# Attention and two gated projections on one core: padding that moves where the SBUF buffers begin

## Chip, cores and metric

The kernel runs on one core of a Trainium2 chip. The metric is the device time of one launch in microseconds (us), the median of the runs shown.

## What is computed

Attention over 2 batches and 8 heads of 768 positions, each position seeing the 31 positions around it and a summary of every block of 32 (the maximum of the block's keys, the mean of its values); then two dense stages, all of it in float32:

```
scores = concat(where(|i-j| < 16, q k^T / 8, -1e9), q max_blocks(k)^T / 8 + log 32)
x  = softmax(scores) @ concat(v, mean_blocks(v))      # 1536 x 512
y  = ((x @ w_a) * (x @ w_b)) @ w_out                  # 512 -> 1536 -> 512
h  = y @ w_in                                         # 512 -> 2048
out = (h - tanh(h)) @ w_out2                          # 2048 -> 512
```

## The kernel before

**Tiles and stages.** The 1536 tokens are three blocks (`NBLK`) of `TB` = 512. Batch 0's attention is written out operation by operation in the list `SEQ` (a head of some 40 us, run by `op`); batch 1's attention is spread by a plan (`plan`, `run_plan`) between the matmuls of the first dense stage. The program is then a list of positions, `pos`: for each block and each of the 12 slices of the first hidden layer, `pos_a` (x @ w_a), `pos_b` (x @ w_b) and `pos_o` (the product @ w_out), and for each block and each of the 16 slices of the second hidden layer `pos_h` (y @ w_in and the function h - tanh h) and, two positions later, `pos_o2` (its product with w_out2). Every position is one unit of 12 matmuls: 4 pieces of 128 by 3 products, since each float32 number is held as a high and a low part (`hi_lo`, `split_w`) and high*high, high*low and low*high are added up. So there are 36 units each of `pos_a`, `pos_b` and `pos_o`, and 48 each of `pos_h` and `pos_o2`.

**What a matmul reads.** Both operands lie in SBUF; one is loaded as weights (stationary, 128 columns, 512 bytes in a partition), the other streams through (moving, 512 columns, 2048 bytes).

- `proj` (L370; called by `pos_a`, `pos_b`, `pos_h`): stationary from `wsp`, moving from `XA` or `XB`.
- `pos_o` (L398): stationary from `wsp`, moving from `gh` or `gl`.
- `pos_o2` (L459): stationary from `gh` and `gl` in two units of three and from `vw` in the third (`G % 3`), moving from `wsp`.

**Who feeds them.** Weights arrive by DMA in `stage` (or `x21a`, `x21b`, `qbd`), are rebuilt by ACT, POOL and DVE into `w` (L154 to L165, L179) and split into `wsp` (L184, L185). SP issues all DMAs in the order of the program. The order on each engine follows the program's order and the tile framework's scheduler.

**Where a buffer lies.** All SBUF buffers come from one pool, `sb`, through `st(shape, tag, bufs)`. They lie one behind the other in the order in which their tags are first asked for, each start rounded up to 32 bytes. A tag with n buffers takes n places side by side. So a start is set by everything that was asked for before it: the row of constants at the front (three masks of 480 bytes, `mavg` of 176 and so on) sets the start of all that follow, the 12,672 bytes of `kt` shift what stands behind them, and the eight small tiles `nm` and `sm` (16 bytes each, first asked for between `e` and `ta` of the first softmax) shift the last ones.

Of the kernel before, what the change touches and what calls it, by code (L numbers as in the profile page):

```python
# [39 lines left out]
def band_attention_moe_kernel(ctx: ExitStack, tc: tile.TileContext, q, k, v, w_a, w_b, w_out, w_in, w_out2, out):  # L40
# [22 lines left out]
    def st(shape, tag, bufs=1, dt=F32):  # L63
        return sb.tile(shape, dt, tag=tag, bufs=bufs, name=tag)

    def pt(tag, shape=(128, 512)):
        return ps.tile(list(shape), F32, tag=tag, name=tag)
# [4 lines left out]
    bsq = st([128, 1], "bsq")  # L72
    bth = st([128, 1], "bth")
    mavg = st([128, 2 * NB - 4], "mavg")
    mavp = st([128, KW + 2 * NB - 8], "qn", 3)
    qbd = st([128, 2, NP, 128], "qbd")
    qbd2 = st([128, 2, NP, 128], "wsp", 4)
# [6 lines left out]
    def constants():  # L84
        nc.vector.memset(bsq, -math.sqrt(GA) * GB)
        nc.vector.memset(bth, -GC2)
        nc.vector.memset(qbd2, 0.0)
        nc.gpsimd.memset(qbd3, 0.0)

        for m, n, r in ((mavp, KW + 2 * NB - 8, BLK // 2), (mavg, 2 * NB - 4, BLK)):  # L90
            nc.gpsimd.memset(m, 1.0 / BLK)
            nc.gpsimd.affine_select(
                out=m, in_=m, pattern=[[-r, n]], compare_op=ALU.is_gt, fill=0.0,
                base=(n - NB) * r + 1, channel_multiplier=1,
            )
            nc.gpsimd.affine_select(
                out=m, in_=m, pattern=[[r, n]], compare_op=ALU.is_gt, fill=0.0,
                base=r - (n - NB) * r, channel_multiplier=-1,
            )
        nc.gpsimd.memset(qbd4, 0.0)  # L100
        for m, off in zip(masks, (0, WIN, 2 * WIN)):
            nc.gpsimd.memset(m[:, 0:KW], 0.0)
            nc.gpsimd.memset(m[:, KW:NK], math.log(BLK) / SC)
            for h in range(2):
                band = m[h * 64 : h * 64 + 64, 0:KW]
                nc.gpsimd.affine_select(
                    out=band, in_=band, pattern=[[1, KW]], compare_op=ALU.is_gt, fill=NEG,
                    base=WIN - off, channel_multiplier=-1,
                )
                nc.gpsimd.affine_select(  # L110
                    out=band, in_=band, pattern=[[-1, KW]], compare_op=ALU.is_gt, fill=NEG,
                    base=WIN + off, channel_multiplier=1,
                )
# [491 lines left out]
    def op(n):  # L605
        import re
        k, a = re.match("([A-Za-z]+)(.*)", n).groups()
        i = int(a[0]) if a and a[0].isdigit() else 0
# [14 lines left out]
        elif k == "Kt":  # L623
            i = int(a)
# [4 lines left out]
        elif k == "Ke":  # L629
            i = int(a)  # L630
# [9 lines left out]
        elif n.startswith("T1t"):  # L640
            i = int(n[3])
# [5 lines left out]
        elif n.startswith("T1e"):  # L647
            i, o = int(n[3]), "ab".index(n[4])
# [16 lines left out]
        elif k == "tt":  # L665
            b, w, k0 = where(i)
            e = st([128, NP, NK], ("e", "ta", "tg")[i // 2], 2) if i < 6 else st([128, NP, NK], "w", 36)
            nm = st([128, NP], "nm", 4)
            sm = st([128, NP], "sm", 4)
            mk = masks[0 if w == 0 else 1]  # L670
            for p in range(NP):
                nc.vector.tensor_tensor_reduce(
# [18 lines left out]
        elif n.startswith("T3t"):  # L691
            i = int(n[3])
# [5 lines left out]
        elif n.startswith("T3e"):  # L698
            i = int(n[3])
# [3 lines left out]
        elif n.startswith("T4m"):  # L703
            i = int(n[3])
# [9 lines left out]
        elif n.startswith("T4"):  # L714
            i = int(n[3])
# [57 lines left out]
    with tc.manual_schedule():  # L773
        nc.vector.memset(qbd, 0.0)
        for _ in range(WARM):
            mm(pt("ps")[:, 0:256], qbd[:, 0, 0, :], qbd[:, 0, 0:2, :], start=True, stop=True)
        make_identity(nc, ident)
        XAv = st([128, 4, 2 * TB], "XA")
        kt[0] = st([128, NP, S + NB], "kt")
        constants()  # L780
        for n in SEQ.split():
            exec(compile(f"def op_{n}(op): op('{n}')\n", "<ops>", "exec"), globals())
            globals()["op_" + n](op)
# [50 lines left out]
```

## Time and profile before

| | |
|---|---|
| runs | 667.33, 665.36, 667.28 us; median 667.28 |
| span of the profiled execution, first to last instruction | 664.0 us |
| median less that span | 3.3 us |
| busy: PE, DVE, ACT, POOL | 643.2, 501.9, 476.2, 209.7 us |
| TensorE clock granted, mean | 0.997 of full speed |
| DMA moved | 62.1 MB |

PE is TensorE's matmuls, PEld its weight loads, which overlap them; DVE is VectorE, ACT ScalarE, POOL GpSimd, SP the engine that issues DMAs (SPq its sequencer). The chain of waits is the work that ended last, followed back from the last instruction; a row of it gives the start, the length and the instructions of a piece, and a run of matmuls stands in it by the time from its first start to the next piece's start. A group's row gives busy time, mean ns of one, and the idle time ahead. [...]

### The profile page before, as it was taken

To read this page: it belongs to the slowest core of one execution; us is meant where nothing else is said; L and a number is where in the kernel's file an instruction comes from. 1 tells how busy PE (TensorE), PEld (TensorE's weight loads), DVE (VectorE), ACT (ScalarE), POOL (GpSimd) and SP (SyncE) were. 2 spreads that over 40 slices of the span, in tenths; PEclk is the share of its full clock that TensorE was granted. 3 is DMA by queue.
4 is the path that set the end of the run, shared out by engine and by line. 5 is a ranking of instruction groups with operands and counts; after the bars stand their busy time and mean duration, and the time that the engine had idled before them with its cause. 6 is when DMAs were issued, how large, how long until landed. Compare 5 with 4: busy or idle time off the path is not lost.

```text
span 664.0 us, 9626 instructions
## 1 busy us (share of the span) xinstructions
PE 643.2 (97%) x3240; PEld 518.1 (78%) x3240; DVE 501.9 (76%) x999; ACT 476.2 (72%) x1000; POOL 209.7 (32%) x221
## 2 busy tenths in 40 slices
PE   7778999999899999999999999999999999999997
PEld 5567876888588888888888888888888888888885
DVE  5899999888675777647877748877777877777775
ACT  4899897798677687636655547777777777777774
POOL 6761231122000010101111135554444544444441
PEclk9989999999999999999999999999999999999999
DMA  9996984563414545513444200000010000000001
GB/s 203 243 237 179 250 226 128 169 216 107 102 66 124 169 152 155 144 47 112 149 140 152 68 1 0 1 0 1 1 63 1 0 1 0 32 33 1 1 0 64
DMA packets 84781, 62.11 MB, mean 94 GB/s; under 512 B 51892, under 2 KB 75444, under 8 KB 84732
## 3 DMA queue, kind: packets, MB, share of 16 engines
q1 hardware_dynamic: 84732, 61.50, 33.4%
q8 instruction: 25, 0.41, 0.3%
q14 instruction: 24, 0.20, 0.1%
HBM read 54.00 MB, written 7.34 MB: 92 GB/s over the span
## 4 chain that ended last, share of the span: by engine, by line
PE 82%; DVE 7%; ACT 4%; DMA 3%; issue 2%; SPq 1%; POOL 0%; DVEq 0%; ACTq 0%
PE acc L459 20%; PE pb L370 18%; PE pa L370 17%; PE acc L398 12%; PE pt L370 5%; PE ps L370 5%; DMA stage<-in_moe_w_in_dram 2%; PE ps L288 1%; DVE w L164 1%; PE ps L340 1%; DVE w L165 1%; PE pt L240 1%; PE pt L327 1%; DMA x20a<-in_q_dram 1%; SPq L610 1%
## 5 line engine op out<-in xcount | busy, mean ns | idle before, releaser
L185 POOL TENSOR_TENSOR wsp<-w,wsp 128x512 fp32r<-128x512 f32 x97 | 127.5, 1333 | 143.7 <-ACT wsp L184 143.7
L184 ACT ACTIVATE wsp<-w 128x512 fp32r<-128x512 f32 x201 | 121.4, 622 | 18.8 <-PE acc L398 8.6
L185 DVE TENSOR_TENSOR wsp<-w,wsp 128x512 fp32r<-128x512 f32 x104 | 75.0, 723 | 42.5 <-ACT wsp L184 42.3
L179 POOL TENSOR_SCALAR w<-w 128x512 f32<-128x512 f32 x52 | 42.0, 811 | 184.3 <-ACT w L154 184.1
L398 PE MATMUL acc<-gh,wsp 128*128 128x512 f32 x288 | 97.8, 398 | 0.5 <-ACT gh L363 0.5
L370 PE MATMUL pa<-XA,wsp 128*128 128x512 f32 x336 | 85.0, 400 | 2.8 <-ACT XA L720 2.1
L370 PE MATMUL pb<-XA,wsp 128*128 128x512 f32 x336 | 84.1, 394 | 1.4 <-DVE tg L386 1.4
L459 PE MATMUL acc<-wsp,gh 128*128 128x512 f32 x256 | 80.5, 396 | 0.0
L370 PEld LDWEIGHTS pa<-XA,wsp 128*128 128x128 f32 x336 | 63.5, 191 | 18.3 <-ACT XA L720 2.4
L370 PEld LDWEIGHTS pb<-XA,wsp 128*128 128x128 f32 x336 | 62.1, 188 | 15.0 <-ACT x21a L155 1.6
L363 ACT ACTIVATE gh<-tg 128x512 fp32r<-128x512 f32 x68 | 42.4, 623 | 33.3 <-DVE tg L386 32.9
L398 PEld LDWEIGHTS acc<-gh,wsp 128*128 128x128 f32 x288 | 53.7, 188 | 12.0 <-ACT gh L363 0.6
L370 PE MATMUL pb<-XB,wsp 128*128 128x512 f32 x240 | 61.0, 396 | 0.0
L370 PE MATMUL pa<-XB,wsp 128*128 128x512 f32 x240 | 60.4, 395 | 0.0
L398 PE MATMUL acc<-gl,wsp 128*128 128x512 f32 x144 | 57.3, 399 | 1.1 <-DVE gl L364 1.1
L459 PEld LDWEIGHTS acc<-wsp,gh 128*128 128x128 f32 x256 | 48.2, 188 | 11.1
L364 DVE TENSOR_TENSOR gl<-tg,gh 128x512 fp32r<-128x512 f32 x68 | 46.6, 686 | 9.4 <-ACT gh L363 9.3
L370 PEld LDWEIGHTS pa<-XB,wsp 128*128 128x128 f32 x240 | 44.5, 188 | 9.8 <-DVE XB L348 0.2
L370 PEld LDWEIGHTS pb<-XB,wsp 128*128 128x128 f32 x240 | 44.4, 188 | 9.5
L459 PE MATMUL acc<-wsp,gl 128*128 128x512 f32 x128 | 50.5, 394 | 0.0
L459 PE MATMUL acc<-wsp,vw 128*128 128x512 f32 x192 | 46.5, 390 | 0.0
L459 PEld LDWEIGHTS acc<-wsp,vw 128*128 128x128 f32 x192 | 35.9, 188 | 8.1 <-DVE vw L364 0.4
(304 smaller groups left out, 1176.0 us busy)
## 6 DMA issues: line engine op xcount, KB each, us to landing
stage<-in_moe_w_out_dram SPq DMA_DIRECT2D x19, 512.0 KB, 3.8
stage<-in_moe_w_in_dram SPq DMA_DIRECT2D x16, 512.0 KB, 5.6
stage<-in_moe_w_a_dram SPq DMA_DIRECT2D x8, 512.0 KB, 4.9
w<-wsc SPq DMA_DIRECT2D x16, 256.0 KB, 3.5
vw<-in_v_dram SPq DMA_DIRECT2D x19, 192.0 KB, 3.2
stage<-in_moe_w_b_dram SPq DMA_DIRECT2D x7, 512.0 KB, 5.7
wsc<-x21a SPq DMA_DIRECT2D x8, 256.0 KB, 4.9
wsc<-x21b SPq DMA_DIRECT2D x8, 256.0 KB, 5.1
```

Of the source, the lines that this page charges most:

```text
L164: nc.vector.scalar_tensor_tensor(r, t[:, :, 1], -0x40000000, r, op0=ALU.bitwise_and, op1=ALU.bitwise_or)
L165: nc.vector.tensor_tensor(r, r, t[:, :, 0], op=ALU.add)
L179: nc.gpsimd.tensor_scalar(rf, rf, HI_HI, HI_LO, op0=ALU.min, op1=ALU.max)
L184: nc.scalar.activation(s[:, 0, :], r, AF.Copy)
L185: eng.tensor_tensor(s[:, 1, :], r, s[:, 0, :].bitcast(F32), op=ALU.subtract)
L240: mm(pp, mavg[:, NB - 4 - 4 * c : 2 * NB - 4 - 4 * c], vch.pop(c).rearrange("p h d -> p (h d)"), start=(c == 0), stop=(c == NC - 1),)
L288: mm(pp[:, p, 0:NK], qt[:, p, :], kw[:, p, :], start=True, stop=True)
L363: nc.scalar.activation(dst[0], src, AF.Copy)
L364: eng.tensor_tensor(dst[1], src, dst[0].bitcast(F32), op=ALU.subtract)
L370: mm(dst, w, xx, start=(kk == 0 and n == 0), stop=(kk == KC - 1 and n == 2))
L398: mm(acc[blk][d][:, c0:c1], w, t, start=(f == 0 and c0 == 0 and n == 0), stop=(f == F1 - 1 and n == 2))
L459: mm(a[c], g[:, cs], s[:, i, :], start=(f == 0 and n == 0), stop=(f == F2 - 1 and n == 2))
```

## The change

Three tiles are asked for that nothing writes or reads: 52, 64 and 32 words of 4 bytes in a partition. They stand behind `mavg`, behind the first `nm` and `sm` of the third softmax (by then `ta` has its place, `tg` not), and behind `kt`.

```diff
     mavg = st([128, 2 * NB - 4], "mavg")
+    st([128, 52], "pad0")
     mavp = st([128, KW + 2 * NB - 8], "qn", 3)
@@ in op(), "tt"
             nm = st([128, NP], "nm", 4)
             sm = st([128, NP], "sm", 4)
+            if i == 2:
+                st([128, 64], "pad2")
             mk = masks[0 if w == 0 else 1]
@@ ahead of the head
         kt[0] = st([128, NP, S + NB], "kt")
+        st([128, 32], "pad1")
         constants()
```

The first byte of each buffer in its partition, from the two built programs, with its rest modulo 512 (of tags with several buffers the first; the others follow at multiples of 2048 or 4096, so with the same rest):

| tags in the order of the pool | before | rest | after | rest |
|---|---|---|---|---|
| `ident`, masks, `mavg` | 16512 to 18528 | mixed | unchanged | mixed |
| `qn`, `qbd` | 18720, 24864 | 288 | 18944, 25088 | 0 |
| `wsp` (4 of 4096) | 28960 | 288 | 29184 | 0 |
| `XB`, `kw`, `w` | 45344, 61728, 65824 | 288 | 45568, 61952, 66048 | 0 |
| `vw` (3 of 2048) | 139552 | 288 | 139776 | 0 |
| `XA`, `kt` | 145696, 162080 | 288 | 145920, 162304 | 0 |
| `x20a`, `x20b`, `stage` | 174752, 178848, 182944 | 160 | 175104, 179200, 183296 | 0 |
| `x21a`, `x21b`, `e` | 195232, 199328, 203424 | 160 | 195584, 199680, 203776 | 0 |
| `ta` | 207776 | 416 | 208128 | 256 |
| `tg` | 211872 | 416 | 212480 | 0 |
| `gh`, `gl`, `at` | 215968, 220064, 224160 | 416 | 216576, 220672, 224768 | 0 |

The instructions, their order and what each waits for are the same in the two built programs on all engines; only addresses differ.

## Rows read from the trace of the kernel before

**Rows 1.** The page's head: span, busy time (share of the span), instructions, and the chain.
```profile
span 664.0 us, 9626 instructions
...
PE 643.2 (97%) x3240; PEld 518.1 (78%) x3240; DVE 501.9 (76%) x999; ACT 476.2 (72%) x1000; POOL 209.7 (32%) x221
...
PE 82%; DVE 7%; ACT 4%; DMA 3%; issue 2%; SPq 1%; POOL 0%; DVEq 0%; ACTq 0%
```

**Rows 2.** Busy time (instructions) by stage: PE PEld DVE ACT POOL, clock, DMA share, GB/s.
```profile
0.00:60.00 60.00, 46.36 (x343) 35.27 (x344) 48.02 (x153) 46.37 (x138) 34.09 (x64) 0.97 1.03 229
...
114.00:182.00 68.00, 64.82 (x374) 52.02 (x373) 55.69 (x129) 53.30 (x124) 12.59 (x15) 1.00 0.51 149
182.00:280.00 98.00, 98.00 (x568) 80.01 (x567) 70.01 (x183) 72.45 (x184) 9.94 (x14) 1.00 0.46 137
280.00:395.00 115.00, 115.00 (x518) 94.02 (x517) 77.58 (x121) 60.86 (x108) 17.20 (x20) 1.00 0.29 99
395.00:655.00 260.00, 260.00 (x1133) 212.66 (x1132) 196.75 (x300) 196.23 (x346) 122.25 (x93) 1.00 0.02 9
```

**Rows 3.** Groups of L459's matmuls by the tile that is stationary.
```profile
L459 PE MATMUL acc<-wsp,gh 128*128 128x512 f32 x256 | 80.5, 396 | 0.0
...
L459 PE MATMUL acc<-wsp,gl 128*128 128x512 f32 x128 | 50.5, 394 | 0.0
L459 PE MATMUL acc<-wsp,vw 128*128 128x512 f32 x192 | 46.5, 390 | 0.0
```

**Rows 4.** The chain, 386 to 440 us: start, length, engine, tile, line, count.
```profile
386.63 2.72 PE pb L370 x12
389.35 2.79 PE acc L398 x12
392.14 2.73 PE pa L370 x12
...
403.13 2.80 PE acc L459 x12
405.92 2.76 PE pt L370 x12
408.68 2.80 PE acc L459 x12
411.48 2.75 PE pa L370 x12
414.23 2.72 PE acc L459 x12
416.95 2.73 PE pb L370 x12
```

**Rows 5.** The chain, 182 to 280 us: an early unit of L398 that nothing interrupts.
```profile
210.29 2.80 PE acc L398 x12
```

**Rows 6.** L398's matmuls by stage (PE, PEld, clock, DMA share, GB/s).
```profile
114.00:182.00 68.00, 22.04 (x84) 15.32 (x84) 1.00 0.51 149
```

**Rows 7.** Groups of L363 (ACT) and L364 (DVE) by the tile written.
```profile
L364 DVE TENSOR_TENSOR gl<-tg,gh 128x512 fp32r<-128x512 f32 x68 | 46.6, 686 | 9.4 <-ACT gh L363 9.3
...
L363 ACT ACTIVATE gh<-tg 128x512 fp32r<-128x512 f32 x68 | 42.4, 623 | 33.3 <-DVE tg L386 32.9
...
L364 DVE TENSOR_TENSOR vw<-tg,vw 128x512 fp32r<-128x512 f32 x16 | 11.0, 685 | 0.7 <-ACT vw L363 0.7
...
L363 ACT ACTIVATE vw<-tg 128x512 fp32r<-128x512 f32 x16 | 9.9, 618 | 1.8 <-DVE tg L438 1.8
```

**Rows 8.** The chain's DMA pieces, and SP's issues ahead of the first.
```profile
5.02 1.14 SPq L610
...
6.21 1.15 SPq L615
...
7.40 5.14 DMA x20a<-in_q_dram
...
128.25 4.11 DMA stage<-in_moe_w_b_dram
...
156.86 5.63 DMA stage<-in_moe_w_in_dram
...
169.91 4.88 DMA stage<-in_moe_w_in_dram
```

**Rows 9.** DMA issues: tile, source, count, size, median us to landing.
```profile
stage<-in_moe_w_out_dram SPq DMA_DIRECT2D x19, 512.0 KB, 3.8
stage<-in_moe_w_in_dram SPq DMA_DIRECT2D x16, 512.0 KB, 5.6
```

## Prediction

> **What bounds the kernel now.** I read the page's head first: PE is busy 643.2 of 664.0 us and 82% of the chain runs over it [rows 1], so almost the only way to a shorter time is a shorter way through the matmuls. The table by stage then says where PE is the bound and where not [rows 2]. From 182 us on PE is busy in every microsecond. Between 114 and 182 us it has 68.00 - 64.82 = 3.2 us of gaps, and in the first 60 us it has 13.6 us of them while the DMA engines are full (share 1.03) and DVE and ACT busy for 48.0 and 46.4 us. In the stage from 395 to 655 us DVE and ACT are busy for 197 and 196 of 260 us and DMA for 2%: the others have room there if PE gets faster.
>
> The question is then whether a matmul's time depends on where its operands begin, and this trace answers it by itself. `pos_o2` (L459) runs the same matmuls with the stationary operand in `gh` and `gl` in two units of three, and in `vw` in the third. The groups differ: 396 and 394 ns from `gh` and `gl`, 390 ns from `vw` [rows 3]. In the chain, where a unit stands by its cadence, it is clearer: units of 12 take 2.80, 2.80, 2.72 us in turn, and the reader finds the 2.72 us where `G % 3` gives `vw` [rows 4]. Nothing else changes with it: the line, the moving tile `wsp`, the shapes, and the DVE and ACT work of a position are the same in all three.
>
> The table of addresses has what does change. Modulo 512, `wsp`, `XA`, `XB` and `vw` begin at 288, `gh` and `gl` at 416. Every pair of equal rest takes 2.72 to 2.73 us a unit (L370 with `XA` or `XB` against `wsp`; L459 with `vw`), every pair that is 128 bytes apart takes 2.79 to 2.80 us (L398 with `gh` and `gl` moving; L459 with them stationary) [rows 4]. It costs the same 0.07 to 0.08 us whether the 2048-byte or the 512-byte operand is the shifted one, which speaks for the distance between the two, not for the rest of either. Within an L370 unit the stationary slice moves on by 512 bytes four times while the moving one keeps its rest, and the unit is still 2.72 us: steps of 512 do not count. There is an after-effect too: an L370 unit behind a slow L459 unit takes 2.75 to 2.76 us, behind the fast one 2.73.
>
> **The change, part by part.** The pads hold nothing and no instruction names them; order and waits stay. So all that can change is the duration of accesses. After it `wsp`, `XA`, `XB`, `vw`, `gh` and `gl` all have rest 0, so every matmul pair of the two dense stages has distance 0 modulo 512, the fast class of before.
>
> - *L459 from `gh`, `gl`*: 256 + 128 matmuls are 32 units; 32 x (2.80 - 2.72) = 2.6 us, all in the stage that PE bounds from end to end.
> - *L370 behind them*: 32 units x (2.755 - 2.73) = 0.8 us.
> - *L398 from 182 us on and before 114 us*: of 36 units 7 (84 matmuls) lie between 114 and 182 us [rows 6]; an early uninterrupted unit takes the same 2.80 us as the late ones [rows 5], so the price holds there too. 29 x (2.79 - 2.72) = 2.0 us.
> - *L370 behind those*: 29 x (2.73 - 2.72) = 0.3 us.
> - *The 7 units of L398 between 114 and 182 us*: 0.5 us that I cost at nothing. Cover: the chain there runs over DVE, ACT and three loads of `stage` [rows 8]; PE's 3.2 us of gaps grow by it. Without that cover they would give 0.5 us more.
> - *ACT and DVE*: `gl` from `tg`, `gh` (all rest 416) takes 686 ns, `vw` from `tg`, `vw` (416 and 288) 685; ACT's copy into `gh` takes 623 and into `vw` 618 [rows 7]. Rows at different distances agree within 1%, so nothing for these engines; at 5 ns for each of ACT's 68 copies it would be 0.3 us, and not on the path.
> - *DMA*: no row shows a transfer to a start with rest 0 modulo 256. The nearest rows are SP's issues while the DMA engines are full: 1.14 us for a piece of k into `XB` (rest 32 modulo 256) and 1.15 us for one of q into `x20a` (rest 160) [rows 8]; the rest does not show. So I take nothing. Bounds: transfers can hardly get slower by it; at the other end, a load of 512 KB in longer pieces (w_out) lands in 3.8 us against 5.6 [rows 9], so the most that a finer split can cost is 1.8 us a load, and four transfers stand on the chain [rows 8]: 4 x 1.8 = 7.2 us. I keep 0 as one end and 7.2 as the other.
>
> Sum: 2.6 + 0.8 + 2.0 + 0.3 = 5.7 us. The span goes from 664.0 to 658.3 us. The median of the runs is 667.28, 3.3 us over that span, and I leave the 3.3: 667.28 - 5.7 = **661.6 us**, with 659 to 664 as this case's own range (some units meet DVE or DMA in the early stage; a run can lie 2 us off the median, as 665.36 does).
>
> [...] The rows say that a distance of 128 bytes costs 2.79 - 2.72 us a unit. [...]
>
> **Rivals.**
>
> *No change: the slow class is a matter of place, not of alignment.* `gh` and `gl` also stand behind byte 215,000, in the region of `ta`, `tg`, `e` and `at`, which ACT and DVE use all the time, and `vw` does not. Were it this, the units from `gh` and `gl` would stay at 2.80 us, since they stay in that region: 667.3 us. For it: the trace has no tile of that region at rest 288. Against it: ACT is busy for 60.86 of 115 us in the stage from 280 us and for 196 of 260 in the next [rows 2], and the slow unit is 2.79 us in the one and 2.80 in the other [rows 4]; a clash with other engines would follow their work. [...] Chance 0.15.
>
> *Slower: rest 0 for all is worse than rest 288 for most.* If the price depends on where both streams begin, and not on their distance, the 2.72 us of today's units could be a gift of 288, and at 0 all units would run at the slow cadence. Units that would go from 2.72 to 2.80 us: 120 of L370 and 16 of L459, less some 14 between 114 and 182 us, 122 x 0.08 = 9.8 us: 677 us. It decides against the change from 5.7 / 122 = 0.047 us a unit on. Against it: `gh` and `gl` as moving and as stationary operand cost the same, and two streams of so different length would hardly pay the same for a start. Chance 0.09.
>
> *More than forecast: transfers get shorter as well.* The head and the two holes around 130 and 157 to 175 us wait for loads, 19.8 us in four pieces [rows 8], so a faster transfer shows on the path at once. Between 0 and 7.2 us more, so 654 to 661; I put 657 for it. [...] Chance 0.10.
>
> The forecast itself: 0.66.
>
> **How the numbers follow.** About 0.3%, 2 us, is what a measurement of this kernel can tell from no change. Faster: 0.66 + 0.10 = 0.76; the same: 0.15; slower: 0.09. The range goes from 656.5 (half of the case with shorter transfers) to 667.5 (most of the case without change): 0.66 + 0.05 + 0.10, about 0.8.
>
> **What would show it.** Right: in the chain the L459 units all at 2.72 us with no third one apart, L398 at 2.72, L370 behind them at 2.72 to 2.73; the group of L459 from `gh` at 390 ns as that from `vw`; DVE and ACT groups as before; the loads on the chain as long as before. Wrong in place: L459 from `gh` and `gl` still at 396 and 394. Wrong in sign: `pa` and `pb` at 2.80. Wrong in size: the matmuls as forecast, but the chain's DMA pieces shorter, or gaps of PE between 60 and 280 us that take the gain back.

## The result: faster by 0.9%, in the matmuls

The changed kernel takes 660.3 us against 666.79 us before (medians of six runs each). One of its six runs, the one that was profiled, was granted little over half of TensorE's clock throughout (0.56 in the mean, 1067.74 us); it counts in the median and not in the ratio, and the rows of after below come from the second comparison. The ratio is 0.9913, with a 95% interval of 0.9889 to 0.9936. A second comparison of the same two gave 659.34 against 665.36 us, ratio 0.9915 (0.9890 to 0.9940); by that ratio the gain is 5.7 us, with an interval from 4.0 to 7.3. The forecast was 661.6 us, a gain of 5.7. L459 of before is L460 here, L398 is L399, L370 is L371, L363 and L364 are L364 and L365.

The head of the page:

```profile
span 657.4 us, 9626 instructions
...
PE 636.3 (97%) x3240; PEld 518.0 (79%) x3240; DVE 503.1 (77%) x999; ACT 475.2 (72%) x1000; POOL 209.0 (32%) x221
...
PE 84%; DVE 7%; ACT 4%; DMA 2%; issue 1%; POOL 1%; SPq 0%; DVEq 0%; ACTq 0%; POOLq 0%
```

The span is 6.6 us shorter and PE's busy time 6.9 us; DVE, ACT and POOL are busy as long as before within 1.2 us [rows 1]. The groups of L460 by the stationary tile:

```profile
L460 PE MATMUL acc<-wsp,gh 128*128 128x512 f32 x256 | 78.8, 389 | 0.0
...
L460 PE MATMUL acc<-wsp,gl 128*128 128x512 f32 x128 | 49.8, 389 | 0.0
L460 PE MATMUL acc<-wsp,vw 128*128 128x512 f32 x192 | 46.5, 390 | 0.0
```

`gh` and `gl` came down from 396 and 394 ns to 389; `vw` stands at its 390 [rows 3]. (These are recorded durations; from one start to the next it is 226.7 ns, a twelfth of a unit's 2.72 us.) The chain where [rows 4] stood:

```profile
386.34 2.72 PE acc L399 x12
389.06 2.72 PE pa L371 x12
...
397.22 2.72 PE ps L371 x12
399.94 2.72 PE acc L460 x12
402.66 2.72 PE pt L371 x12
405.38 2.72 PE acc L460 x12
408.10 2.72 PE pa L371 x12
410.82 2.72 PE acc L460 x12
```

Every unit is 2.72 us now, and no third one stands apart. (Only the very last one is longer; the part on the prediction comes back to it.) The stage that begins with the first `ps` unit began at 400.40 us before (its row in the same chain, with 263.6 us to the end of the span) and begins at 397.22 now, with 260.2 to the end: 3.4 us of the gain lie behind that point and 3.2 ahead of it.

The stages, in the columns of [rows 2]:

```profile
0.00:60.00 60.00, 45.96 (x347) 35.94 (x348) 48.55 (x154) 46.78 (x139) 34.71 (x64) 0.97 0.86 230
...
114.00:182.00 68.00, 64.89 (x376) 52.28 (x374) 55.73 (x129) 53.00 (x123) 12.31 (x15) 1.00 0.50 153
```

PE's gaps between 114 and 182 us are 3.1 us, and were 3.2. One row moved that was to stay: the DMA share of the first 60 us, 0.86 against 1.03 [rows 2], at 230 GB/s against 229. More on it with the experiments.

### The profile page after: what moved, and what is told of

Same layout as the page of the kernel before. It is cut to its first block, busy times and chain, and to the rows that moved or that the text cites. A ratio compares the mean times of both kernels' runs of the same rounds, so it can differ in the third digit from the quotient of the medians.

```text
span 1066.0 us, 9626 instructions
## 1 busy us (share of the span) xinstructions
PE 1054.9 (99%) x3240; PEld 626.0 (59%) x3240; DVE 500.4 (47%) x999; ACT 486.3 (46%) x1000; POOL 197.3 (19%) x221
## 4 chain that ended last, share of the span: by engine, by line
PE 98%; ACT 1%; DVE 0%; DMA 0%; issue 0%; POOL 0%; ACTq 0%
PE pb L371 21%; PE pa L371 21%; PE acc L460 21%; PE acc L399 15%; PE ps L371 5%; PE pt L371 5%; PE ps L289 2%; PE ps L341 1%; PE pt L328 1%; PE pt L241 1%; PE pt L270 1%; PE pb L732 0%; PE acc L289 0%; DMA stage<-in_moe_w_in_dram 0%; PE acc L699 0%; PE ps L779 0%
## 5 line engine op out<-in xcount | busy, mean ns | idle before, releaser
L399 PE MATMUL acc<-gh,wsp 128*128 128x512 f32 x288 | 147.2, 582 | 0.0
L371 PE MATMUL pa<-XA,wsp 128*128 128x512 f32 x336 | 136.4, 580 | 2.7 <-ACT XA L723 2.5
L371 PE MATMUL pb<-XA,wsp 128*128 128x512 f32 x336 | 137.3, 578 | 0.1
L460 PE MATMUL acc<-wsp,gh 128*128 128x512 f32 x256 | 123.2, 577 | 0.0
L371 PEld LDWEIGHTS pa<-XA,wsp 128*128 128x128 f32 x336 | 74.3, 223 | 56.1 <-issue 29.9
L371 PEld LDWEIGHTS pb<-XA,wsp 128*128 128x128 f32 x336 | 73.4, 222 | 52.9 <-issue 31.2
L371 PE MATMUL pb<-XB,wsp 128*128 128x512 f32 x240 | 99.4, 582 | 0.0
L371 PE MATMUL pa<-XB,wsp 128*128 128x512 f32 x240 | 98.3, 578 | 0.0
L399 PEld LDWEIGHTS acc<-gh,wsp 128*128 128x128 f32 x288 | 64.0, 223 | 42.8 <-issue 24.4
L399 PE MATMUL acc<-gl,wsp 128*128 128x512 f32 x144 | 83.6, 582 | 0.0
L460 PEld LDWEIGHTS acc<-wsp,gh 128*128 128x128 f32 x256 | 56.2, 219 | 42.6 <-issue 25.4
L460 PE MATMUL acc<-wsp,vw 128*128 128x512 f32 x192 | 76.8, 575 | 0.0
L371 PEld LDWEIGHTS pa<-XB,wsp 128*128 128x128 f32 x240 | 52.9, 223 | 36.3 <-issue 21.2
L460 PE MATMUL acc<-wsp,gl 128*128 128x512 f32 x128 | 73.8, 577 | 0.0
L371 PEld LDWEIGHTS pb<-XB,wsp 128*128 128x128 f32 x240 | 52.4, 220 | 36.2 <-issue 21.2
L364 ACT ACTIVATE gh<-tg 128x512 fp32r<-128x512 f32 x68 | 42.3, 623 | 57.9 <-DVE tg L387 57.4
L387 DVE TENSOR_TENSOR tg<-pb,ta 128x512 f32<-128x512 f32 x36 | 24.9, 692 | 91.1 <-PE pb L371 91.1
```

What stands on the lines that cost most here:

```text
L364: nc.scalar.activation(dst[0], src, AF.Copy)
L371: mm(dst, w, xx, start=(kk == 0 and n == 0), stop=(kk == KC - 1 and n == 2))
L387: nc.vector.tensor_tensor(t, p, ab.pop(g), op=ALU.mult)
L399: mm(acc[blk][d][:, c0:c1], w, t, start=(f == 0 and c0 == 0 and n == 0), stop=(f == F1 - 1 and n == 2))
L460: mm(a[c], g[:, cs], s[:, i, :], start=(f == 0 and n == 0), stop=(f == F2 - 1 and n == 2))
```

## The experiments

Two theories stood against the one of the prediction (the **distance** of a matmul's two operands modulo 512 sets its cadence): that starts at **rest 0** are what counts, and that `gh` and `gl` lie in a slow **place**. A third question was what aligned starts do for transfers. The first three runs vary distance and alignment apart from each other. In the kernels of the ladder and of `XB` alone apart, L370, L398 and L459 of before are L372, L400 and L461.

**The changed kernel again** (no edit). 

> The changed kernel once more, for a profile of it. Distance theory (a matmul's cadence is set by the distance of its two operands modulo 512): units of L460 (L459 of before) from gh and gl at 2.72 us as those from vw, units of L399 (L398) at 2.72, L371 (L370) behind them at 2.72 to 2.73; the loads on the chain as long as before; span near 658. Transfer theory (aligned starts shorten DMA): the loads that stood on the chain (4.1 to 5.6 us) shorter by 0.5 us or more each.

Measured: 659.34 us, rows above. The cadences are those of the distance theory. The loads on the chain did not get shorter as a group: 3.89 and 5.90 us in the places of 4.11 and 5.63 [rows 8], the third one no longer on the chain.

```profile
127.13 3.89 DMA stage<-in_moe_w_b_dram
155.86 5.90 DMA stage<-in_moe_w_in_dram
```

**One pad alone, no buffer aligned.**

```diff
--- before
             sm = st([128, NP], "sm", 4)
+            if i == 2:
+                st([128, 96], "pad2")
```

> One pad of 96 words alone, where the second pad stands: gh, gl and at move from rest 416 to rest 288, where wsp, XA, XB and vw stay; no large buffer begins at a multiple of 256. Distance theory: all of the gain without any alignment, 5 to 6.5 us under the kernel before, units of L459 from gh at 2.72 us. Rest-0 theory (the gain comes from starts at multiples of 256): no change, 667. Place theory (the region behind byte 215,000 is slow): no change, 667, L459 from gh at 2.80.

Measured: 660.29 us against 665.36, ratio 0.9916 (0.9897 to 0.9934): all of the gain, with no large buffer at a multiple of 256. Its chain:

```profile
399.07 2.72 PE ps L370 x12
401.79 2.72 PE acc L459 x12
404.51 2.72 PE pt L370 x12
407.23 2.72 PE acc L459 x12
```

So rest 0 is not needed, and the place theory falls too: `gh` and `gl` moved by 384 bytes and stayed in their region. (The profiled span, 659.2 us, is longer than the changed kernel's, 657.4. One part of it is the clock: from 170 to 180 us it was granted 0.83 in the mean, the changed kernel 1.00.)

**Aligned, but 128 bytes apart.**

```diff
--- the changed kernel
             if i == 2:
-                st([128, 64], "pad2")
+                st([128, 96], "pad2")
```

> The changed kernel with a second pad of 96 words in place of 64: all buffers that DMA writes early and all of the first dense stage's at rest 0, but gh, gl and at at rest 128, so 128 bytes from wsp as before. Distance theory: as before within 1.5 us, L459 from gh at 2.80 us and from vw at 2.72. Rest-0 theory and transfer theory: most of the gain stays, 660 to 663. What differs from the kernel before is what alignment by itself does for DMA, ACT and DVE.

Measured: 665.34 us against 665.36, ratio 0.9997 (0.9985 to 1.001): nothing is left of the gain with all buffers but `tg`, `gh`, `gl` and `at` at a multiple of 256. The units of the chain have the lengths of before [rows 4]:

```profile
403.18 2.80 PE acc L460 x12
405.97 2.76 PE pt L371 x12
408.73 2.80 PE acc L460 x12
411.53 2.75 PE pa L371 x12
414.28 2.72 PE acc L460 x12
417.00 2.73 PE pb L371 x12
```

The three runs and the kernel before make a square:

| | distance 128 | distance 0 |
|---|---|---|
| buffers ahead of `tg` at rest 288, 160, 416 | before: 665.36 us, DMA share of the first 60 us 1.03 | one pad: 660.29 us, 1.03 |
| buffers ahead of `tg` at rest 0, 256 | 665.34 us, 0.84 | changed kernel: 659.34 us, 0.86 |

The time follows the column, the DMA share the row. Alignment does help the DMA engines, and no gain in time can be told from it: at distance 128 the ratio with aligned starts is 0.9997, with an interval that leaves room for at most 1.0 us. SP's issues show the help, in the timeline of SP before and then of the changed kernel (start, length, count):

```profile
0.80 5.36 SPq L610 DMA_DIRECT2D XB<-in_k_dram  x6
6.21 2.33 SPq L615 DMA_DIRECT2D x20a<-in_q_dram  x2
```

```profile
0.80 4.80 SPq L611 DMA_DIRECT2D XB<-in_k_dram  x6
5.64 1.99 SPq L616 DMA_DIRECT2D x20a<-in_q_dram  x2
```

The other two runs of the square go with their rows: 5.52 and 2.33 us with the one pad, 5.02 and 2.03 aligned but apart. And the timeline of PE where most of that lead is lost, before and then changed:

```profile
11.37 0.66 PE L645 MATMUL acc<-ident,x20a 128*128 128x128 f32 x4 [0.55 <-DMA x20a<-in_q_dram]
...
13.54 1.12 PE L288 MATMUL pt<-kw,qbd 128*128 128x120 f32 x8 [0.24 <-ACT qbd L599]
```

```profile
9.91 0.60 PE L646 MATMUL acc<-ident,x20a 128*128 128x128 f32 x4
...
13.49 1.12 PE L289 MATMUL pt<-kw,qbd 128*128 128x120 f32 x8 [1.84 <-ACT qbd L600]
```

q is there and being transposed 1.46 us earlier, and the first scores start 0.05 us earlier: PE waits 1.84 us for ACT's `qbd` where it waited 0.24. The chain of the changed kernel has there what took the place of the load, DVE's maximum over the key blocks:

```profile
9.24 0.61 ACT kt L632
...
9.87 1.90 DVE kt L635 x3
```

Some of the lead may reach the first projection (the first matmul of L370). It starts at 42.00 us in the changed kernel, at 42.56 before and at 42.46 with one pad. In the run aligned but apart it starts at 42.95, but there the clock was granted 0.83 in the mean from 10 to 20 us, and 1.00 in the others; the unaligned run with `gl` alone apart (below) has the same 0.83 and 43.28. The ladders and `XB` alone apart (below) start it at 42.18 to 42.49. So with aligned starts it may come 0.2 to 0.6 us earlier; that is less than the times can tell, and it is not shown.

**A ladder of distances.** In three kernels, each measured in a single run, every tile got its own distance from `wsp`, with pads ahead of `XB`, `vw`, `XA`, `tg` and `gl`:

```diff
--- before (first ladder; the others: 40, 8, 8, 8, 16 and 72, 16, 16, 112, 8 words)
+    st([128, 8], "pad3")
     xb = st([128, 2 * KC * TB], "XB")
+    st([128, 8], "pad4")
     vwb = [st([NK, H, D], "vw", 3) for _ in range(3)]
+        st([128, 8], "pad5")
         XAv = st([128, 4, 2 * TB], "XA")
+            if i == 2:
+                st([128, 8], "pad2")
+            if i == 5:
+                st([128, 16], "pad6")
             t = st([NK, NP, 128], ("at", "gh", "gl")[i // 2], 2) if i < 6 ...
```

> Small pads that give each tile its own distance from wsp modulo 512: XB 32, vw 64, XA 96, gh 256, gl 320 (tg goes with gh, at with gl). Distance theory: the cadence is a function of the distance, so L370 units differ between XA and XB and L459 units between vw, gh and gl; those at 256 should be like 0 if only bit 7 counts (2.72 us), and like or worse than 128 if the whole distance below 512 counts. If the price is fixed for any distance but 0, all run at 2.79 to 2.80 us and the time is 10 us over before (677). Place theory: XA, XB and vw stay at 2.72 us.

> Distances from wsp modulo 512: XB 160, vw 192, XA 224, gh 384, gl 448. So far 32, 64, 96, 128, 256 and 320 all ran at 231 to 234 ns from one matmul to the next against 226.7 at 0. Distance theory with a fixed price for any distance but 0: again 231 to 234 ns in all groups, 670 to 673 us. Distance theory with more than one favourable distance: one of these groups at 226.7 or below.

> Distances from wsp modulo 512: XB 288, vw 352, XA 416, gh 480, gl 0. Fixed price for any distance but 0: 231 to 234 ns in all groups whose operands are apart; 669 to 672 us. The units of L459 mix slices of gh at 480 and of gl at 0: if the price is paid by the pair itself, the matmuls with gl run at 226.7 ns and those with gh at 232; if it is paid by what is loaded while the one ahead streams, the fast ones stand one place earlier.

Measured: 671.85, 670.94 and 672.32 us, 5.6 to 7 us over the kernel before. The mean time from one matmul's start to the next, from 300 us on (gaps over 260 ns cut), by the tile that meets `wsp`:

| distance | 0 | 32 | 64 | 96 | 128 | 160 | 192 | 224 |
|---|---|---|---|---|---|---|---|---|
| tile | `XA`, `XB`, `gh`, `gl`, `vw` | `XB` | `vw` | `XA` | `XB` | `XB` | `vw` | `XA` |
| ns | 226.7 | 232.4 | 233.3 | 233.5 | 232.7 | 233.1 | 229.0 | 233.1 |

| distance | 256 | 288 | 320 | 352 | 384 | 416 | 448 | 480 |
|---|---|---|---|---|---|---|---|---|
| tile | `gh` | `XB` | `gl` | `vw` | `gh` | `XA` | `gl` | `gh` |
| ns | 231.5 | 232.7 | 231.7 | 233.0 | 233.0 | 233.8 | 231.7 | 233.0 |

(The value at 0 is the changed kernel's, that at 128 the run below with `XB` alone apart, the others those of the ladders; `gh`, `gl` and `vw` in L461, where units mix two distances for `gh` and `gl`.) Only 0 reads fast; all others cost 2 to 7 ns, most of them 5 to 7, and none is better than 0. For two of them, 320 and 448, the table does not settle it. In the third ladder `gl` is at distance 0, yet its matmuls, between slow ones with `gh`, run at 232.3 ns: a fast pair among slow ones is not fast. At 320 and 448 it was again `gl` among slow `gh`, and 231.7 ns is what a fast distance would read there too. (The reverse would show: where `gl` alone is apart, below, the first `gh` of three runs at 227 ns.) The time came out below the 677 us that was expected of the first ladder: that sum priced all L370 units against 2.72 us, while those behind a slow unit already stood at 2.73 to 2.76.

**Another 512 bytes.**

```diff
--- one pad alone
-                st([128, 96], "pad2")
+                st([128, 224], "pad2")
```

> The pad of the single-pad kernel longer by 512 bytes: gh, gl and at another 512 bytes away from wsp, rest 288 modulo 512 as before it. If the distance counts modulo 512: as the single-pad kernel, L459 from gh at 226.7 ns, 659 to 661 us. If it counts modulo 1024 or more: 232 ns, 665 to 667 us.

Measured: 659.58 us in a single run, and the chain as fast as with the short pad:

```profile
397.66 2.72 PE ps L370 x12
400.38 2.72 PE acc L459 x12
```

So 512 bytes are a whole turn for this pair.

**`XB` alone apart.**

```diff
--- one pad alone
+    st([128, 32], "pad3")
     xb = st([128, 2 * KC * TB], "XB")
+    st([128, 96], "pad4")
     vwb = [st([NK, H, D], "vw", 3) for _ in range(3)]
```

> The single-pad kernel with XB alone moved 128 bytes from wsp (pads ahead of XB and of vw, all others of the dense stages at rest 288). Distance theory: the price moves with the tile. L370 with XB (672 matmuls, 56 units) slow, 0.07 to 0.08 us a unit, 3.9 to 4.5 us in all and up to 1 us of after-effects; L370 with XA, L398 and L459 fast apart from the first matmuls behind an XB unit; 663 to 665 us. Place theory: XB lies where it lay, L370 with XB stays at 2.72 us, 659 to 661.

Measured: 663.62 us against 665.76 before, ratio 0.9961 (0.9947 to 0.9975), 3.3 us over the run with one pad. (`kw` and `w` lie between the two pads and move along; none of the dense stages' matmuls reads them.) The slow class went where the distance went:

```profile
405.10 2.79 PE pt L372 x12
407.89 2.73 PE acc L461 x12
410.63 2.79 PE pa L372 x12
413.42 2.73 PE acc L461 x12
```

L372 with `XB`, fast in the kernel before, is slow, and L461 fast but for its first three matmuls (232, 232, 231 ns, then 227), the after-effect. Behind the first `ps` unit this costs 2.6 us by the spans (262.7 against 260.1 with one pad), and 32 x 0.07 + 32 x 0.01 = 2.6 by these units.

**`gl` alone apart.**

```diff
--- one pad alone
+            if i == 5:
+                st([128, 32], "pad6")
             t = st([NK, NP, 128], ("at", "gh", "gl")[i // 2], 2) if i < 6 ...
```

> The single-pad kernel with gl (and at) alone 128 bytes from wsp: one matmul in three of L398 and of two L459 units in three is apart, the others are not. If each matmul pays for its own pair only: 144 + 128 matmuls x 6.3 ns = 1.7 us, units of 2.74 to 2.75 us, those with gh at 226.7 ns. If the after-effect spoils the next three: the whole units are slow again at 2.79 us, 3 to 5 us over the single-pad kernel.

Measured: 664.32 us in a single run. Its units lie between the two expectations:

```profile
395.32 2.75 PE acc L398 x12
398.07 2.72 PE pb L370 x12
...
403.51 2.77 PE acc L459 x12
406.28 2.72 PE pt L370 x12
409.00 2.77 PE acc L459 x12
...
414.49 2.72 PE acc L459 x12
```

In the timeline (start, length, count) the next matmul starts 0.24 us behind one with `gl`, and two with `gh` take 0.45 us together:

```profile
403.35 0.62 PE L459 MATMUL acc<-wsp,gh 128*128 128x512 f32 x2
403.80 0.40 PE L459 MATMUL acc<-wsp,gl 128*128 128x512 f32 x1
404.04 0.62 PE L459 MATMUL acc<-wsp,gh 128*128 128x512 f32 x2
```

In L398, where `gl` streams, only its own matmul is slow (234 ns, those with `gh` 226.3). In L459, where `gl` is the stationary operand, two of three are: 234 ns with `gl` itself and 232 to 233 ns in the matmul with `gh` just ahead of it, during which the slice of `gl` is loaded (in the trace of before that matmul starts at 403.20 us, the load at 403.21 with 0.19, the matmul with `gl` at 403.44); the other is 227. So the price is not paid by a matmul for its own pair alone: 36 x 0.03 + 32 x 0.05 = 2.7 us by these units. The span is 3.4 us over that of the single-pad kernel (662.6 against 659.2): 1.7 behind the first `ps` unit, 0.9 between the first projection and that unit, and 0.8 ahead of it. The 0.8 goes with the clock more likely than with the distance: from 10 to 20 us TensorE was granted 0.83 in the mean here and 1.00 there.

## Why the prediction was right, and where it was not

- **Distance as the cause.** Right, and shown: the one pad gets all of the gain, aligned starts at the old distance get none that can be told, and `XB` becomes slow when it alone is moved.
- **L459 from `gh` and `gl`, 2.6 us, and L370 behind them, 0.8.** Right per unit: 2.80 to 2.72 us, and 2.755 to 2.72 behind them. By the chain the stage gave 3.4 us, the sum that was forecast, but that is partly luck. The L370 term was too small: 2.73 was assumed where 2.72 came, so it is 1.1 us. The L459 term was too large: two of its 32 units gave nothing in the end. The last three units take 8.75 us in the chain of before and 5.44 + 0.03 + 3.31 = 8.78 us in that of the changed kernel, because the last unit waits for ACT to write `vw`: its first weights stand 0.45 us idle for that in place of 0.30. By the starts of the matmuls a unit went from 2.796 to 2.720 us, and 30 x 0.076 are 2.3.
- **L398, 2.0 us, and L370 behind it, 0.3.** Right in size per unit, 2.79 to 2.72; ahead of the stage the spans differ by 3.2 us in place of 2.3. Of what is over, 0.6 us lies ahead of the first projection (42.0 us in place of 42.6, see above). Between the first projection and the stage the gain is 2.6 us, in the changed kernel as with the longer single pad (355.2 us each, 357.8 before). The third load that left the chain explains none of it: it is off the chain in the run aligned but apart too, which gained nothing.
- **The 7 units between 114 and 182 us at nothing.** Perhaps too low. PE's gaps there went from 3.2 to 3.1 us and did not grow by 0.5 us. By the starts of ACT's copies into `ta`, the changed kernel leads by 0.9 us at 114 us and by 1.2 at 181; with the longer single pad it is 0.1 and 0.8. The run aligned but apart, which gained nothing, is 0.3 us behind at 114 us and 0.1 at 181, so this is little above the noise. Some of the 0.5 us may have come through (0.3 is also what is missing between 2.3 and 2.6); that is not shown, and it was not tried apart.
- **ACT and DVE at nothing.** Right: ACT's copies into `gh` and `vw` take 623 and 616 ns where they took 623 and 618, DVE's `gl` and `vw` 687 and 685 where they took 686 and 685 [rows 7]; the groups of the changed kernel:

```profile
L364 ACT ACTIVATE gh<-tg 128x512 fp32r<-128x512 f32 x68 | 42.4, 623 | 33.5 <-DVE tg L387 33.1
...
L365 DVE TENSOR_TENSOR gl<-tg,gh 128x512 fp32r<-128x512 f32 x68 | 46.7, 687 | 9.6 <-ACT gh L364 9.4
...
L365 DVE TENSOR_TENSOR vw<-tg,vw 128x512 fp32r<-128x512 f32 x16 | 11.0, 685 | 0.7 <-PE acc L460 0.7
...
L364 ACT ACTIVATE vw<-tg 128x512 fp32r<-128x512 f32 x16 | 9.9, 616 | 1.8 <-DVE tg L439 1.8
```

- **DMA at nothing.** Right for the time, as far as 0.9997 with alignment alone can tell, wrong in the reason. "The rest does not show" was read from rests of 32 and 160, which are equally slow at 1.14 and 1.15 us a piece [rows 8]; rest 0 was not in the trace and is faster: six pieces of k in 4.80 us of issues in place of 5.36, two of q in 1.99 in place of 2.33. In these issues only the starts on the written side moved. That transfers can hardly get slower was my estimate, which no row showed: these got faster, and of the two loads of `stage` left on the chain one took 3.89 us in place of 4.11, the other 5.90 in place of 5.63. What hides most of the gain in the head is the next wait, DVE's 1.90 us on the keys.
- **The rivals.** No change, by place: fell, with 0.9916 from a pad that aligned nothing. Slower at rest 0: fell, all units at 2.72. Shorter transfers: the pieces of k and q got shorter, the loads of `stage` on the chain did not as a group, and no time was gained by it that can be told (0.9997).

## What to carry to other kernels

Here a unit of 12 matmuls back to back went from 2.80 to 2.72 us when its stationary and its moving tile got starts that are equal modulo 512 bytes, and one pad of 384 bytes was the whole cost; whether it is so in another kernel, its own trace has to show. One cause is found by looking within one line of the trace for two groups that differ in the tile alone. A resource that gets faster (here DMA in the head, with q there 1.46 us earlier) is worth only what the next wait on the chain leaves of it (0.05 us at the first scores), so the chain is read again behind such a change. And a price that was read from units waits for the stage's end: the last units can give it back in a wait for another engine (here the last three took 8.78 us in place of 8.75).

## What the runs showed of the hardware

- Matmuls of 128x512 on the high and low parts of float32 followed each other every 226.7 ns, at a granted clock of 1.00, where both operands began at the same place modulo 512 bytes, and every 229 to 234 ns at 13 other distances tried in steps of 32 bytes; 320 and 448 could not be told apart from their slow neighbours. Finer distances were not tried, and what inside the engine makes the difference stays open.
- A slow unit left its mark on the three matmuls behind it in the run with `XB` alone apart (232, 232, 231 ns, then 227), even though their own operands fit. A single slow stationary operand slowed the matmul ahead of it too (232 to 233 ns where `gl` alone is apart, against 227).
- DMA into starts at multiples of 256 bytes kept the DMA engines busy for 0.84 to 0.86 of the first 60 us where other starts took 1.03, for the same bytes, 0.88 of them in pieces of 256 bytes to 1 KB (in the trace of before). A piece of 256 bytes took 18.0 ns in the mean over the trace in place of 22.1.
